# Sliding-window attention with a feed-forward stage: weights loaded and decoded in 16 parts of 1024 columns instead of 32 parts of 512

## The chip, the cores and the metric

One core of a Trainium2 chip runs the kernel. The metric is device time in microseconds (us) of one execution; lower is better. The engines of the core are TensorE (PE, with its weight loads PEld), VectorE (DVE), ScalarE (ACT), GpSimd (POOL) and SyncE (SP); here SP only issues DMAs, in order, and a DMA that waits holds back all that stand behind it on SP.

## The reference

```python
# attention, B=4, H=8, S=768, D=64, n_sink=4, window=128
scores = scale * np.matmul(q, k.transpose(0, 1, 3, 2))
keep = is_sink | in_window                       # rel = query - key, 0 <= rel < window
scores = np.where(keep, scores, -1000000000.0)
a = softmax(scores)
x = (a @ v).transpose(0, 2, 1, 3).reshape(3072, 512)
# feed-forward, d_model 512, d_ff 2048
h = x @ w_in
g = h * np.clip(h + 3.0, 0.0, 6.0) / 6.0
out = g @ w_out                                  # 3072 x 512 float32
```

The two weights w_in (512 x 2048) and w_out (2048 x 512) come as 64-bit floats, and the kernel itself turns each number into two 32-bit halves, a rounded high part and the rest (hi and lo).

## The kernel before

**Units.** A unit is one batch and 256 queries; there are 12 (4 batches, 3 stretches of queries). In the list `pus` each unit stands with each of its 4 pairs of heads, 48 entries s in all. The first stretches of all batches come first (entries 0 to 15). The first 12 entries are plain: they multiply in one pass and need no split keys. From entry 12 on keys and queries are split and stacked: `B_k` writes the split keys to `kt` and copies them by four DMAs into the tile `K`, of which there is one.

**The slot loop.** For each s the string ORDER lists what the program issues: the loads of V (`V`), the scores of entry s-1 (`C0`, `C1`: PE sp, then DVE line 320), the product with V of entry s-2 (`E0`, `E1`: PE av), exp (`X`, ACT line 341), the loads of keys and queries two entries ahead (`L`), the normalisation (`N`, lines 328 and 330), `Bk`, `Bq`, the weights (`W`), and the transposes (`D0`, `D1`: PE pt, ACT pf). At every `-` one step of the feed-forward stage is drained from `queues`. I call one turn of this loop a slot.

**The feed-forward stage.** When all four pairs of a unit are done, 34 steps are queued. For each of 8 groups i of 256 hidden columns: two halves of `ffn1` (PE hps, line 461; behind the second half ACT line 467, DVE lines 468, 41 and 470 make gf, gh and g), and two `ffn2` (PE o, line 481). A step is only issued when the weights of its group have been issued.

**The weights.** Group i needs `WIH[i]`, `WIL[i]` (from w_in) and `WOH[i]`, `WOL[i]` (from w_out), which stay in SBUF. `load_part` fetches one part by a DMA into a buffer st, and decodes it by a chain that changes engine three times: ACT line 153 (st to wt) and line 157 (st in place), DVE line 159 (st in place) and line 161 (wt from wt and st, after which st is free), ACT line 35 (hi from wt) and DVE line 164 (lo from wt and hi, after which wt is free). There are 32 parts of 128 x 512 numbers, 512 KB each, four for each group. st has four buffers (three with the tag st and one with the tag vs), wt three. WN says how many parts each slot issues: 1 in each of slots 1 to 4, 4 in each of slots 5 to 11. The result tile ost of `ffn_out` shares the tag st.

The order of instructions on each engine is fixed when the kernel is built, by a scheduler that works on the program's order and its own costs; on the chip each engine runs its list in order.

Of the kernel before, what the change touches and what calls it, by code (L numbers as in the profile page):

```python
# [9 lines left out]
F32 = mybir.dt.float32  # L10
F32R = mybir.dt.float32r
I32 = mybir.dt.int32
# [6 lines left out]
P = 128  # L19
# [7 lines left out]
def split_parts(nc, hi, lo, src, hi_engine, lo_engine):  # L27

    copy_r(nc, hi_engine, hi, src)
    lo_engine.tensor_tensor(out=lo, in0=src, in1=hi.bitcast(F32), op=ALU.subtract)  # L30


def copy_r(nc, eng, out, src, scale=1.0):
    if eng is nc.scalar:
        nc.scalar.mul(out=out, in_=src, mul=scale)  # L35
    elif eng is nc.gpsimd:
        nc.gpsimd.tensor_scalar(out=out, in0=src, scalar1=scale, scalar2=1.0, op0=ALU.mult, op1=ALU.mult)
    elif scale != 1.0:
        nc.vector.tensor_scalar(out=out, in0=src, scalar1=scale, scalar2=None, op0=ALU.mult)
    else:  # L40
        nc.vector.tensor_copy(out=out, in_=src)  # L41
# [3 lines left out]
def attn_ffn_kernel(ctx: ExitStack, tc: tile.TileContext, qx, kx, vx, vfx, vsx, n_sink, window, w_in, w_out, out):  # L45
    nc = tc.nc
    B, NU, NP = qx.shape[0:3]
    NT, DM = out.shape
    NFP = w_in.shape[0]
# [7 lines left out]
    work = fast.enter_context(tc.tile_pool(name="work", bufs=2))  # L57
# [66 lines left out]
    WIH = [const.tile([P, NP, 256], F32R, name=f"wih{i}") for i in range(NFP)]  # L124
    WIL = [const.tile([P, NP, 256], F32R, name=f"wil{i}") for i in range(NFP)]
    WOH = [const.tile([P, 2, DM], F32R, name=f"woh{i}") for i in range(NFP)]
    WOL = [const.tile([P, 2, DM], F32R, name=f"wol{i}") for i in range(NFP)]
# [3 lines left out]
    def weng(which, at):  # L131
        return {"D": nc.vector, "P": nc.gpsimd, "A": nc.scalar}[which[at % len(which)]]

    def load_part(hi, lo, src, rows, at):

        def like(t):
            return t.rearrange("p (a b) -> p a b", a=rows)

        if not wide:
            st = like(work.tile([P, 512], F32, tag="st", name="st", bufs=3))  # L140
            nc.sync.dma_start(out=st, in_=src)
            split_parts(nc, hi, lo, st, nc.scalar, nc.vector)
            return

        tag, bufs = ("vs", 1) if at % 4 == 3 else ("st", 3)
        st = work.tile([P, 512, 2], I32, tag=tag, name="st", bufs=bufs)
        it = work.tile([P, 512], I32, tag="wt", name="wt", bufs=3)
        nc.sync.dma_start(out=like(st.rearrange("p n w -> p (n w)")), in_=src.bitcast(I32))
        low, high = st[:, :, 0], st[:, :, 1]
        ft = it.bitcast(F32)  # L150


        nc.scalar.activation(out=ft, in_=high.bitcast(F32), func=AF.Abs, scale=2.0 ** -112)

        nc.scalar.activation(out=low, in_=low.bitcast(U32), func=AF.Copy, scale=2.0 ** -29 * (1 - 2.0 ** -18),  # L157
                             bias=7.5 * 2.0 ** -18 - 0.5)
        nc.vector.scalar_tensor_tensor(out=low, in0=high, scalar=-2 ** 31, in1=low,
                                       op0=ALU.bitwise_and, op1=ALU.bitwise_or)  # L160
        nc.vector.scalar_tensor_tensor(out=it, in0=it, scalar=3, in1=low,
                                       op0=ALU.logical_shift_left, op1=ALU.bitwise_or)
        copy_r(nc, weng(WHI, at), hi, like(ft))
        weng(WLO, at).tensor_tensor(out=lo, in0=like(ft), in1=hi.bitcast(F32), op=ALU.subtract)  # L164

    def load_w_in(i, c):
        cs = slice(2 * c, 2 * c + 2)
        load_part(WIH[i][:, cs, :], WIL[i][:, cs, :], w_in[i, :, cs, :], 2,
                  4 * i + c)

    def load_w_out(i, c):
        cs = slice(c, c + 1)
        load_part(WOH[i][:, cs, :], WOL[i][:, cs, :], w_out[i, :, cs, :], 1,
                  4 * i + 2 + c)

# [28 lines left out]
    def eng(which, s):  # L206
        return {"D": nc.vector, "P": nc.gpsimd, "A": nc.scalar}[which[1 + (s % (len(which) - 1)) if s < START else 0]]
# [242 lines left out]
    def ffn1(x, i, pool, psum, half, state, tag):  # L450

        if half == 0:
            state["h"] = psum.tile([P, 2, UT], F32, tag=tag or "hps", name="hps")
        hp = state["h"]
        fs = slice(P * half, P * (half + 1))
        n = 3 * NP
        j = 0
        for c in range(NP):
            xh, xl = x[c]
            for l, r in ((WIH[i][:, c, fs], xh), (WIH[i][:, c, fs], xl), (WIL[i][:, c, fs], xh)):  # L460
                nc.tensor.matmul(out=hp[:, half, :], lhsT=l, rhs=r, start=(j == 0), stop=(j == n - 1))  # L461
                j += 1
        if half == 1:
            g = pool.tile([P, 2, UT], F32R, tag="g", name="g", bufs=2)
            gh = pool.tile([P, 2, UT], F32R, tag="gh", name="gh", bufs=2)
            gf = pool.tile([P, 2, UT], F32, tag="gf", name="gf", bufs=2)
            nc.scalar.activation(out=gf, in_=hp, func=AF.Relu, bias=three, scale=1.0)  # L467
            nc.vector.scalar_tensor_tensor(out=gf, in0=gf, scalar=6.0, in1=hp, op0=ALU.min, op1=ALU.mult)  # L468
            copy_r(nc, eng(GHI, state["n"] * NP), gh, gf)
            eng(GLO, state["n"] * NP).tensor_tensor(out=g, in0=gf, in1=gh.bitcast(F32), op=ALU.subtract)  # L470
            state[i] = (gh, g)

    def ffn2(i, tt, psum, state, tag):
        if i == 0:
            state[f"o{tt}"] = psum.tile([P, DM], F32, tag=tag or f"o{tt}", name=f"o{tt}")
        gh, gl = state[i]
        acc = state[f"o{tt}"]
        ts_ = slice(P * tt, P * (tt + 1))
        for f in range(2):
            for j, (l, r) in enumerate(((gh, WOH), (gh, WOL), (gl, WOH))):  # L480
                nc.tensor.matmul(out=acc, lhsT=l[:, f, ts_], rhs=r[i][:, f, :],  # L481
                                 start=(i == 0 and f == 0 and j == 0),
                                 stop=(i == NFP - 1 and f == 1 and j == 2))

    def ffn_out(tt, pool, state, dst):
        o = pool.tile([P, DM], F32, tag="st", name="ost", bufs=3)
        nc.scalar.mul(out=o, in_=state[f"o{tt}"], mul=1.0 / 6.0)
        nc.sync.dma_start(out=dst, in_=o)

    def ffn_steps(n, x, pool, psum_h, psum_o, dsts, tag=None):  # L490

        state = {"n": n}
        steps = []
        for i in range(NFP + 1):
            if i < NFP:
                for half in range(2):
                    steps.append((4 * i + 2, lambda i=i, half=half: ffn1(x, i, pool, psum_h, half, state, tag)))
            if i >= 1:
                for tt in range(2):
                    steps.append((4 * i, lambda i=i, tt=tt: ffn2(i - 1, tt, psum_o, state, tag)))  # L500
        steps.append((0, lambda: ffn_out(0, pool, state, dsts[0])))
        steps.append((0, lambda: ffn_out(1, pool, state, dsts[1])))
        return steps
# [5 lines left out]
    def drain(n):  # L509

        for _ in range(n):
            live = [q for q in queues if q]
            if not live:
                return
            if live[0] is queues[0] and len(live) > 1:
                order = live[0:2]
            else:
                order = live[0:1]
            for q in order:
                if q[0][0] <= 4 * NFP - len(w_order):  # L520
                    q.pop(0)[1]()
                    break

    w_order = []
    for i in range(NFP):
        for c in range(2):
            w_order.append(lambda i=i, c=c: load_w_in(i, c))
        for c in range(2):
            w_order.append(lambda i=i, c=c: load_w_out(i, c))

    PRE = 0
    for _ in range(PRE):
# [6 lines left out]
    def slot_E(s, h):  # L539
        if 0 <= s < NS:  # L540
            E_av(s, h)
            b, u, p = pus[s]
            if h == 1 and p == NP - 1:
                r0 = b * S + u * UT
                dsts = [out[r0 + P * tt:r0 + P * (tt + 1), :] for tt in range(2)]
                queues.append(ffn_steps(units.index((b, u)), xt[(b, u)], work, ps, ps, dsts, "bank"))

    ORDER = "V C0 - C1 E0 X - E1 L - N - Bk - Bq W - D0 - S D1 -"
    MULT = [1] * 12
    WN = [0, 1, 1, 1, 1, 4, 4, 4, 4, 4, 4, 4]  # L550

    for s in range(NS + 2):
        if s == 3:
            later_constants()
        for step in ORDER.split():
# [23 lines left out]
            elif step == "W":  # L579
                for _ in range(WN[s] if s < len(WN) else 0):  # L580
                    with ExitStack() as behind:
                        if s <= 5:
                            at = max(min(s, NP) - 2, 0)
# [176 lines left out]
```

## Time and profile before

| | |
|---|---|
| median of 3 runs | 748.91 us (747.79 to 750.85) |
| the profiled execution | 751.12 us, its span 749.3 us |
| PE | 727.1 us busy, 97% of the span |
| DVE | 477.9 us busy, 64% |
| ACT | 445.9 us busy, 60% |
| DMA, HBM read | 42.21 MB over the span |

The profiled execution is 2.2 us above the median; 1.8 us of it lie outside its span. Busy times are unions: matmuls overlap in the array, so PE counts as busy while a single late matmul drains. A row of the timeline gives the start, the duration, the engine, the line, what it writes and reads, the shape and how many were merged; in brackets stands how long the engine had been idle before and what released it. [...]

### The profile page before, as it was taken

The numbers are of one execution on the slowest core, as the hardware profiler recorded it, in microseconds if no ns is written. First come the engines' busy times: TensorE is split into PE (matmuls) and PEld (weight loads), VectorE is DVE, ScalarE is ACT, GpSimd is POOL, SyncE is SP. The second block draws the span as 40 slices with busy tenths as digits, with TensorE's granted clock in tenths as the row PEclk, the third lists the DMA queues.
The fourth block names the chain that finished last, engine by engine and source line by source line (L and its number), as shares of the span: only waits on it lengthen the run. The fifth ranks groups of instructions, "written<-read, shape, count | busy, mean of one in ns | idle before, by whom it ended". The sixth has DMA issues, their size and how long they took to land.

```text
span 749.3 us, 13811 instructions
## 1 busy us (share of the span) xinstructions
PE 727.1 (97%) x4932; PEld 653.4 (87%) x4932; DVE 477.9 (64%) x1306; ACT 445.9 (60%) x1099; POOL 4.0 (1%) x17
## 2 busy tenths in 40 slices
PE   8998999999999999999999999999999999999996
PEld 7776878999989998988999889999899889999895
DVE  5798986467767657666756766765766675533321
ACT  6989886556667566666556665756655754411111
POOL 1000000000000000000000000000000000000000
PEclk9999999999999999999999999999999999999999
DMA  7666654336445355345434535535534532000000
GB/s 241 194 205 220 199 173 106 110 81 155 112 123 166 87 127 155 101 114 156 105 98 131 141 101 132 156 87 131 151 102 103 154 83 59 30 1 1 29 1 32
DMA packets 53549, 87.25 MB, mean 116 GB/s; under 512 B 8160, under 2 KB 36320, under 8 KB 53472
## 3 DMA queue, kind: packets, MB, share of 16 engines
q1 hardware_dynamic: 53328, 86.28, 41.9%
q8 instruction: 41, 0.67, 0.4%
q14 instruction: 36, 0.29, 0.1%
q10 hardware_dynamic: 144, 0.00, 0.0%
HBM read 42.21 MB, written 6.29 MB: 65 GB/s over the span
## 4 chain that ended last, share of the span: by engine, by line
PE 69%; ACT 12%; DVE 10%; DMA 5%; issue 2%; SPq 1%; ACTq 0%; DVEq 0%
PE o L481 28%; PE hps L461 27%; PE av L423 5%; PE pt L365 4%; PE sp L313 3%; ACT Pt L328 2%; ACT Pt L341 2%; DMA st<-in_w_in_dram 2%; ACT Ph L341 1%; DVE gf L468 1%; DVE g L470 1%; ACT gf L467 1%; DMA K<-kt 1%; DVE Pt L320 1%; ACT st L157 1%
## 5 line engine op out<-in xcount | busy, mean ns | idle before, releaser
L461 PE MATMUL hps<-xh,wih 128*128 128x256 f32 x768 | 221.0, 288 | 3.6 <-ACT wih L35 3.3
L461 PE MATMUL hps<-xh,wil 128*128 128x256 f32 x768 | 218.0, 284 | 0.0
L461 PE MATMUL hps<-xl,wih 128*128 128x256 f32 x768 | 216.9, 282 | 0.1
L481 PE MATMUL o<-woh,gh 128*128 128x512 f32 x384 | 155.9, 406 | 5.6 <-DVE rc L344 2.3
L481 PE MATMUL o<-woh,g 128*128 128x512 f32 x384 | 153.1, 399 | 1.4 <-DVE g L470 0.9
L461 PEld LDWEIGHTS hps<-xh,wih 128*128 128x128 f32 x768 | 145.0, 189 | 8.9 <-ACT wih L35 6.3
L481 PE MATMUL o<-wol,gh 128*128 128x512 f32 x384 | 151.6, 395 | 0.0
L461 PEld LDWEIGHTS hps<-xl,wih 128*128 128x128 f32 x768 | 145.2, 189 | 2.0 <-issue 0.3
L461 PEld LDWEIGHTS hps<-xh,wil 128*128 128x128 f32 x768 | 145.1, 189 | 0.8 <-DVE wil L164 0.3
L468 DVE SCALAR_TENSOR_TENSOR gf<-gf,hps 128x512 f32<-128x512 f32 x96 | 65.9, 687 | 101.8 <-ACT gf L467 100.7
L467 ACT ACTIVATE gf<-hps,three 128x512 f32<-128x512 f32 x96 | 65.4, 681 | 91.7 <-PE hps L461 91.3
L341 ACT ACTIVATE Pt<-Pt,nb 128x272 f32<-128x272 f32 (+2 forms) x144 | 73.4, 510 | 59.9 <-DVE nb L320 58.5
L481 PEld LDWEIGHTS o<-woh,g 128*128 128x128 f32 x384 | 72.3, 188 | 22.4 <-DVE g L470 5.9
L481 PEld LDWEIGHTS o<-woh,gh 128*128 128x128 f32 x384 | 72.7, 189 | 18.0 <-DVE gh L41 3.4
L481 PEld LDWEIGHTS o<-wol,gh 128*128 128x128 f32 x384 | 72.7, 189 | 10.9
L328 ACT ACTIVATE Pt<-Pt,rc 128x272 f32<-128x272 f32 (+2 forms) x144 | 66.0, 506 | 18.4 <-DVE rc L344 18.3
L470 DVE TENSOR_TENSOR g<-gf,gh 128x512 fp32r<-128x512 f32 x96 | 66.1, 689 | 1.4
L320 DVE CUSTOM_DVE_ANT_0 Pt<-sp,m_t 128x272 f32<-128x272 f32 x128 | 52.3, 438 | 20.7 <-PE sp L313 19.9
L30 DVE TENSOR_TENSOR pl<-pt,ph 128x512 fp32r<-128x512 f32 (+1 forms) x72 | 48.4, 674 | 16.8 <-ACT ph L35 16.3
L35 ACT ACTIVATE ph<-pt 128x512 fp32r<-128x512 f32 (+1 forms) x72 | 42.1, 585 | 19.5 <-PE pt L365 17.2
L313 PE MATMUL sp<-K,Q 128*128 128x272 f32 (+2 forms) x288 | 47.3, 288 | 0.4 <-DMA Q<-qt 0.4
L313 PEld LDWEIGHTS sp<-K,Q 128*128 128x128 f32 x288 | 42.2, 189 | 3.6 <-DMA Q<-qt 0.6
(92 smaller groups left out, 927.9 us busy)
## 6 DMA issues: line engine op xcount, KB each, us to landing
K<-kt SPq DMA_DIRECT2D x128, 200.0 KB, 3.5
Q<-qt SPq DMA_DIRECT2D x144, 64.0 KB, 2.5
st<-in_w_in_dram SPq DMA_DIRECT2D x16, 512.0 KB, 4.0
st<-in_w_out_dram SPq DMA_DIRECT2D x16, 512.0 KB, 5.0
kr<-in_kx_dram SPq DMA_DIRECT2D x32, 200.0 KB, 2.5
qr<-in_qx_dram SPq DMA_DIRECT2D x48, 128.0 KB, 2.2
out_dram<-ost SPq DMA_DIRECT2D x24, 256.0 KB, 2.1
vr<-in_vx_dram SPq DMA_DIRECT2D x32, 192.0 KB, 2.6
```

What stands on the lines that cost most here:

```text
L30: lo_engine.tensor_tensor(out=lo, in0=src, in1=hi.bitcast(F32), op=ALU.subtract)
L35: nc.scalar.mul(out=out, in_=src, mul=scale)
L313: nc.tensor.matmul(out=sp[g][:, 0:w], lhsT=d["Q"][:, g, ts], rhs=d["K"][:, g, part, ks], start=(part == 0), stop=(part == 1))
L320: d["min"] = nc.vector.tensor_tensor_reduce(out=cell(s, g, t, 0, w), in0=sp[g][:, 0:w], in1=m[:, 0:w], scale=-SCALE, scalar=3.0e38, op0=AL ...
L328: nc.scalar.mul(out=blk, in_=blk, mul=c)
L341: d["exp"] = nc.scalar.activation(out=blk, in_=blk, func=AF.Exp, scale=-1.0, bias=d["nb"][:, i:i + 1], accum_out=d["sm"][:, i:i + 1])
L423: nc.tensor.matmul(out=o, lhsT=l, rhs=r, start=(j == 0 and (h == 0 or not plain(s))), stop=(j == len(seq) - 1 and (h == 1 or not plain(s))))
L461: nc.tensor.matmul(out=hp[:, half, :], lhsT=l, rhs=r, start=(j == 0), stop=(j == n - 1))
L467: nc.scalar.activation(out=gf, in_=hp, func=AF.Relu, bias=three, scale=1.0)
L468: nc.vector.scalar_tensor_tensor(out=gf, in0=gf, scalar=6.0, in1=hp, op0=ALU.min, op1=ALU.mult)
L470: eng(GLO, state["n"] * NP).tensor_tensor(out=g, in0=gf, in1=gh.bitcast(F32), op=ALU.subtract)
L481: nc.tensor.matmul(out=acc, lhsT=l[:, f, ts_], rhs=r[i][:, f, :], start=(i == 0 and f == 0 and j == 0), stop=(i == NFP - 1 and f == 1 and ...
```

## The change

The weights come in 16 parts of 128 x 1024 numbers, 1 MB each, two for each group (`load_w_in(i)` and `load_w_out(i)`). Each decode instruction works on 1024 columns and there are half as many. st has two buffers: one with the tag st (the w_in parts) and one in the place of the tile `K` (the w_out parts). wt has three buffers of double size: two with the tag wt and one with the tag vs. ost goes to the tag wt. WN and the conditions for draining count parts of the new size: slot 1 issues w_in of group 0, slot 3 w_out of group 0, slots 5 to 11 both parts of groups 1 to 7.

```diff
+        tag = ("st", "K")[at % 2]
         if not wide:
-            st = like(work.tile([P, 512], F32, tag="st", name="st", bufs=3))
+            st = like(work.tile([P, 1024], F32, tag=tag, name="st", bufs=1))
...
-        tag, bufs = ("vs", 1) if at % 4 == 3 else ("st", 3)
-        st = work.tile([P, 512, 2], I32, tag=tag, name="st", bufs=bufs)
-        it = work.tile([P, 512], I32, tag="wt", name="wt", bufs=3)
+        wtag, bufs = ("vs", 1) if at % 3 == 2 else ("wt", 2)
+        st = work.tile([P, 1024, 2], I32, tag=tag, name="st", bufs=1)
+        it = work.tile([P, 1024], I32, tag=wtag, name="wt", bufs=bufs)
...
-    def load_w_in(i, c):
-        cs = slice(2 * c, 2 * c + 2)
-        load_part(WIH[i][:, cs, :], WIL[i][:, cs, :], w_in[i, :, cs, :], 2,
-                  4 * i + c)
-
-    def load_w_out(i, c):
-        cs = slice(c, c + 1)
-        load_part(WOH[i][:, cs, :], WOL[i][:, cs, :], w_out[i, :, cs, :], 1,
-                  4 * i + 2 + c)
+    def load_w_in(i):
+        load_part(WIH[i], WIL[i], w_in[i], NP, 2 * i)
+
+    def load_w_out(i):
+        load_part(WOH[i], WOL[i], w_out[i], 2, 2 * i + 1)
...
-        o = pool.tile([P, DM], F32, tag="st", name="ost", bufs=3)
+        o = pool.tile([P, DM], F32, tag="wt", name="ost", bufs=2)
...
-                    steps.append((4 * i + 2, lambda i=i, half=half: ffn1(x, i, pool, psum_h, half, state, tag)))
+                    steps.append((2 * i + 1, lambda i=i, half=half: ffn1(x, i, pool, psum_h, half, state, tag)))
...
-                    steps.append((4 * i, lambda i=i, tt=tt: ffn2(i - 1, tt, psum_o, state, tag)))
+                    steps.append((2 * i, lambda i=i, tt=tt: ffn2(i - 1, tt, psum_o, state, tag)))
...
-                if q[0][0] <= 4 * NFP - len(w_order):
+                if q[0][0] <= 2 * NFP - len(w_order):
...
-    WN = [0, 1, 1, 1, 1, 4, 4, 4, 4, 4, 4, 4]
+    WN = [0, 1, 0, 1, 0, 2, 2, 2, 2, 2, 2, 2]
```

The file is three lines shorter behind this place: the decode lines 153, 157, 159, 161 and 164 become 154, 158, 160, 162 and 165, and later lines lose three (341 becomes 338, 328 becomes 325, 461 becomes 458).

The start of ACT's list before, from the first exp of entry 0 to the first hi of the weights (wih; Ph are the scores, pf the transposed ones):

```order
L341 ACTIVATE Ph,sm<-Ph,nb 128x256
L153 ACTIVATE wt<-st 128x512
L328 ACTIVATE Ph<-Ph,rc 128x256 x2
L157 ACTIVATE st<-st 128x512
L35 ACTIVATE pf<-pt 128x384 x2
L153 ACTIVATE wt<-st 128x512
L341 ACTIVATE Ph,sm<-Ph,nb 128x128
L35 ACTIVATE wih_111<-wt 128x512
```

The same place with the change:

```order
L338 ACTIVATE Ph,sm<-Ph,nb 128x256
L154 ACTIVATE wt<-st 128x1024
L325 ACTIVATE Ph<-Ph,rc 128x256 x2
L158 ACTIVATE st<-st 128x1024
L35 ACTIVATE pf<-pt 128x384 x2
L338 ACTIVATE Ph,sm<-Ph,nb 128x128 x2
L338 ACTIVATE Ph,sm<-Ph,nb 128x256
L35 ACTIVATE wih_111<-wt 128x1024
```

The first decode step stands at the same place, ahead of the normalisation of entry 0 (line 328, now 325), and now needs the whole first 1 MB; the second L153 of this stretch has left it, and three of the next four exps stand ahead of the first hi.

A stretch of the load stage on ACT before, group 4 (wih_115 and woh_131 are the high parts of its w_in and w_out), behind the exps of its slot:

```order
L153 ACTIVATE wt<-st 128x512
L157 ACTIVATE st<-st 128x512
L153 ACTIVATE wt<-st 128x512
L328 ACTIVATE Ph<-Ph,rc 128x256 x2
L35 ACTIVATE wih_115<-wt 128x512
L157 ACTIVATE st<-st 128x512 x2
L153 ACTIVATE wt<-st 128x512
L35 ACTIVATE wih_115<-wt 128x512
L35 ACTIVATE pf<-pt 128x384 x2
L157 ACTIVATE st<-st 128x512
L153 ACTIVATE wt<-st 128x512
L35 ACTIVATE woh_131<-wt 128x512 x2
```

The same slot on ACT with the change, from the two exps that open it to its last hi:

```order
L338 ACTIVATE Ph,sm<-Ph,nb 128x128 x2
L154 ACTIVATE wt<-st 128x1024
L464 ACTIVATE gf<-hps,three 128x512
L338 ACTIVATE Ph,sm<-Ph,nb 128x256 x2
L35 ACTIVATE xh_842<-av 128x256
L158 ACTIVATE st<-st 128x1024
L325 ACTIVATE Ph<-Ph,rc 128x256 x2
L154 ACTIVATE wt<-st 128x1024
L158 ACTIVATE st<-st 128x1024
L35 ACTIVATE wih_115<-wt 128x1024
L35 ACTIVATE pf<-pt 128x384 x2
L35 ACTIVATE woh_131<-wt 128x1024
```

And on DVE in the same slot, the decode of group 4 (wil_123 and wol_139 are the low parts):

```order
L160 SCALAR_TENSOR_TENSOR st<-st 128x1024
L162 SCALAR_TENSOR_TENSOR wt<-wt,st 128x1024
L160 SCALAR_TENSOR_TENSOR st<-st 128x1024
L165 TENSOR_TENSOR wil_123<-wt,wih_115 128x1024
L162 SCALAR_TENSOR_TENSOR wt<-wt,st 128x1024
L317 ISA Ph,nb<-sp,m_100 128x128
L317 ISA nb 128x1
L317 ISA Ph,nb<-sp,m_100 128x128
L317 ISA nb 128x1
L165 TENSOR_TENSOR wol_139<-wt,woh_131 128x1024
```

Before, ACT's list of a slot held twelve decode steps of 512 columns between the same rows of attention, those of four parts in turn, so that one part's steps stood between another's; now it holds six of 1024, and on ACT only the two pf stand between the hi of w_in and that of w_out, which needs DVE's second L162.

## Rows read from the trace of the kernel before

**Rows 1.** From the page: the chain of work that ended last, shares of the span by engine and by line.

```profile
PE 69%; ACT 12%; DVE 10%; DMA 5%; issue 2%; SPq 1%; ACTq 0%; DVEq 0%
PE o L481 28%; PE hps L461 27%; PE av L423 5%; PE pt L365 4%; PE sp L313 3%; ACT Pt L328 2%; ACT Pt L341 2%; DMA st<-in_w_in_dram 2%; ACT Ph L341 1%; DVE gf L468 1%; DVE g L470 1%; ACT gf L467 1%; DMA K<-kt 1%; DVE Pt L320 1%; ACT st L157 1%
```

**Rows 2.** Busy time by stretch. Columns: the stretch, its length, busy us and instructions of PE, PEld, DVE, ACT and POOL in this order, the granted clock, the DMA share and GB/s.

```profile
20.00:40.00 20.00, 18.16 (x129) 15.02 (x128) 16.52 (x53) 19.96 (x56) 0.00 (x0) 1.00 0.61 189
...
60.00:80.00 20.00, 18.73 (x109) 15.08 (x109) 18.08 (x45) 18.53 (x43) 0.00 (x0) 0.91 0.62 204
80.00:100.00 20.00, 19.27 (x132) 16.91 (x130) 18.03 (x46) 18.03 (x44) 0.00 (x0) 1.00 0.60 199
...
120.00:140.00 20.00, 20.00 (x124) 16.89 (x123) 10.64 (x35) 12.04 (x35) 0.95 (x1) 1.00 0.38 107
```

**Rows 3.** The start: SP's issue of the first two weight loads, the time from issue to landing of the loads issued from 4.8 to 5.3 us (two) and of the one issued at 6.23 us (the fourth), and ACT's first decode step and PE's first transposes in the timeline.

```profile
4.91 0.80 SPq L148 DMA_DIRECT2D st<-in_w_in_dram  x2
DMA to landing us min/median/max: 5.1/5.6/6.2
DMA to landing us min/median/max: 7.8/7.8/7.8
10.32 0.64 ACT L153 ACTIVATE wt<-st 128x512 f32<-128x512 f32 x1
11.30 1.03 PE L365 MATMUL pt<-ident_r,Ph 128*128 128x128 f32 x6 [0.81 <-DVE Ph L330]
```

**Rows 4.** Timeline, decode steps back to back, first on ACT, then on DVE.

```profile
36.80 0.70 ACT L157 ACTIVATE st<-st 128x512 int32<-128x512 uint32 x1
37.38 0.69 ACT L153 ACTIVATE wt<-st 128x512 f32<-128x512 f32 x1
37.95 0.68 ACT L157 ACTIVATE st<-st 128x512 int32<-128x512 uint32 x1
38.51 0.62 ACT L35 ACTIVATE wih<-wt 128x512 fp32r<-128x512 f32 x1
39.03 0.87 ACT L35 ACTIVATE pf<-pt 128x384 f32<-128x384 f32 x2
39.77 0.69 ACT L157 ACTIVATE st<-st 128x512 int32<-128x512 uint32 x1
...
38.60 0.69 DVE L159 SCALAR_TENSOR_TENSOR st<-st 128x512 int32<-128x512 int32 x1
39.20 0.69 DVE L164 TENSOR_TENSOR wil<-wt,wih 128x512 fp32r<-128x512 f32 x1
39.81 0.69 DVE L161 SCALAR_TENSOR_TENSOR wt<-wt,st 128x512 int32<-128x512 int32 x1
```

**Rows 5.** Groups of instructions from 26 to 113 us with shapes kept apart. Columns: line, engine, operation, names, shapes, count, busy us, mean ns, idle time before them and its releasers.

```profile
L35 ACT ACTIVATE wih<-wt 128x512 fp32r<-128x512 f32 x13 | 8.1, 621 | 0.0
L35 ACT ACTIVATE xh<-av 128x256 fp32r<-128x256 f32 x6 | 2.2, 370 | 0.0
L164 DVE TENSOR_TENSOR wil<-wt,wih 128x512 fp32r<-128x512 f32 x13 | 9.0, 690 | 3.0 <-ACT wih L35 3.0
L439 DVE TENSOR_TENSOR xl<-av,xh 128x256 fp32r<-128x256 f32 x6 | 2.5, 413 | 0.0
```

**Rows 6.** Timeline of ACT, the other work of a slot back to back (exps of 128 and 256 columns, xh, normalisation).

```profile
30.87 0.40 ACT L341 ACTIVATE Ph<-Ph,nb 128x128 f32<-128x128 f32 x1
...
31.25 0.51 ACT L341 ACTIVATE Ph<-Ph,nb 128x256 f32<-128x256 f32 x1
...
31.74 0.51 ACT L341 ACTIVATE Ph<-Ph,nb 128x256 f32<-128x256 f32 x1
...
32.24 0.37 ACT L35 ACTIVATE xh<-av 128x256 fp32r<-128x256 f32 x1
32.50 0.66 ACT L157 ACTIVATE st<-st 128x512 int32<-128x512 uint32 x1
33.05 0.91 ACT L328 ACTIVATE Ph<-Ph,rc 128x256 f32<-128x256 f32 x2
33.85 0.68 ACT L153 ACTIVATE wt<-st 128x512 f32<-128x512 f32 x1
```

**Rows 7.** Timeline of ACT, the fifth and the thirteenth of the sixteen hi steps of w_in, which are the first ones of groups 2 and 6.

```profile
49.29 0.62 ACT L35 ACTIVATE wih<-wt 128x512 fp32r<-128x512 f32 x1
...
99.57 0.62 ACT L35 ACTIVATE wih<-wt 128x512 fp32r<-128x512 f32 x1
```

**Rows 8.** Loads: the page's row on the w_in loads (issues, KB each, median us to landing), the landing of the one load issued from 58.5 to 60 us, and SP's longest wait up to 135 us (total us, times, longest).

```profile
st<-in_w_in_dram SPq DMA_DIRECT2D x16, 512.0 KB, 4.0
DMA to landing us min/median/max: 6.1/6.1/6.1
SPq L148 <- DVE wt L161: 42.5, 21, 4.0
```

**Rows 9.** A gap of PE in the timeline, and busy time by stretch of 2 us around it (columns as in Rows 2).

```profile
59.02 0.47 PE L481 MATMUL o<-woh,gh 128*128 128x512 f32 x1 [2.33 <-DVE rc L344]
...
62.00:64.00 2.00, 2.00 (x8) 1.44 (x7) 2.00 (x4) 2.00 (x6) 0.00 (x0) 0.56 0.10 33
64.00:66.00 2.00, 2.00 (x15) 1.51 (x15) 2.00 (x5) 1.80 (x5) 0.00 (x0) 1.00 0.73 249
```

**Rows 10.** Timeline of DVE at the end of the load stage: the last L161, then the low part of the first split keys.

```profile
120.00 0.69 DVE L161 SCALAR_TENSOR_TENSOR wt<-wt,st 128x512 int32<-128x512 int32 x1
120.60 0.42 DVE L30 TENSOR_TENSOR kt<-kr,kt 128x256 fp32r<-128x256 f32 x1
```

More of the change, by code (lines that the diff above doesn't have):

```diff
@@ L525, in attn_ffn_kernel @@
     for i in range(NFP):
[L526 to L529, printed above, removed]
+        w_order.append(lambda i=i: load_w_in(i))
+        w_order.append(lambda i=i: load_w_out(i))
     PRE = 0
```

## The prediction

> **What bounds the kernel now.** I read the page first, then busy time by stretch, the waits, and the timelines of ACT, DVE and SP up to 130 us. The chain that ended last is 69% PE, nearly all of it the two feed-forward products [rows 1]. From 120 us on PE is never idle, while DVE and ACT are idle nearly half the time [rows 2]: the weights are decoded by then, and nothing in the change touches that work. What is left is the load stage, from 5 to about 120 us. There ACT is full first (19.96 of 20 us from 20 to 40), and then ACT and DVE are both busy 18 of 20 us [rows 2]. PE looks busy there too, but a late matmul counts until it has drained, and it does only 109 matmuls in a stretch of 20 us where 124 fit later. So I take the end time as the moment at which the weights and the first units are ready, plus a remainder that does not change: each us by which the load stage ends earlier or later is a us of the total.
>
> **What an instruction of 1024 columns costs.** Back to back, ACT starts a decode step of 512 columns every 0.57 us (36.80 to 37.38 to 37.95), a hi every 0.52, DVE a step every 0.60, though each lasts longer, 0.62 to 0.69 [rows 4]: the end of one lies under the start of the next. Per column I take the difference between 256 and 512 columns: (621 - 370)/256 = 0.98 ns on ACT, (690 - 413)/256 = 1.08 ns on DVE [rows 5]. 512 columns are thus 0.50 us of ACT's 0.57 and 0.55 of DVE's 0.60. The other steps run at about 1.04 ns a column if the pitch has little else in it. I take a pitch of 1.10 (ACT decode), 1.03 (hi) and 1.13 (DVE), and a duration 0.1 longer. One merged step then saves ACT some 0.03 us and DVE 0.07. Over 48 merges that is 1.4 and 3.4 us of engine time; per slot of six merges 0.2 and 0.4.
>
> [...]
>
> **The start: later.** The first two loads were issued at 4.91 and 5.28 us and landed 5.1 and 6.2 us later, at 10.0 and 11.5; the fourth, issued at 6.23, landed at 14.0 [rows 3]. They come one behind the other, about 1.35 us for 512 KB. With the change the first 1 MB is what the first two loads were: it lands at 11.5. ACT was ready for its first decode step at 10.32 [rows 3] and now waits 1.2 us, with the normalisation of entry 0 (line 325) and so PE's first transposes (11.30) behind it. Then the first hi: ACT reaches it after L158, two pf and three exps, at about 16.7 us by the pitches of [rows 4, 6]. DVE needs L160 and L162 behind L158 with an exp's score between them, 14.6 + 1.2 + 0.3 + 1.2 = 17.3. That is another 0.6 to 0.7 us. ACT has no other idle time up to 40 us to hide this in [rows 2]. Against it stand about 12 merges up to there, 12 x 0.03 = 0.4. The start costs 1.2 + 0.7 - 0.4 = 1.5 us.
>
> **A slot: the same.** I walk one slot with the lists of the change, from the end of ACT's L158 on w_in (time 0).
> - DVE: L160, L162, at 2.4 done; st of w_in is free.
> - ACT meanwhile: normalisation 0.80, L154 and L158 of w_out 2.2, so 3.0; hi of w_in from 3.0 to 4.1, two pf to 4.8.
> - DVE: L160 of w_out can start at 3.1, lo of w_in at 4.3, L162 of w_out at 5.4, done 6.7.
> - ACT: the hi of w_out must wait for it, from 4.8 to 6.7 (idle 1.9), and ends at 7.8.
> - ACT: two exps of 128 columns (0.385 each) to 8.5, L154 of the next w_in to 9.6, Relu 0.57 to 10.2, two exps of 256 (0.49) to 11.2, xh 0.27, L158 from 11.45 to 12.65.
>
> So 12.65 us a slot. Before, group 2 to group 6 took (99.57 - 49.29)/4 = 12.57 us a slot, waits included [rows 7]. The saved pitches are eaten by the hi of w_out, which has no other part's steps to fill its wait. Five such slots make +0.4 us; in the last two slots two units' feed-forward steps share the engines and PE is nearly full (19.27 of 20 us [rows 2]), and I count nothing. Bounds: if the work alone counts, -0.4 x 7 = -2.9; upwards, the load. A w_in part's buffer is free at 2.4 and its next contents are wanted at 8.5, so a load has 6.1 us. 512 KB of w_in landed in 4.0 us in the median [rows 8], so 1 MB is 4.0 + 1.35 = 5.4 us, 0.7 to spare. From the slowest load of that stage, 6.1 [rows 8], it is 7.5, which would cost 1.4 us in a slot.
>
> **What else moves.** On SP a load of weights holds keys, queries and V behind it as before (SP waited 42.5 us for L161 [rows 8]); keys are fetched two entries, some 25 us, ahead, and that covers it. The tile K is free when the last L162 is done. Before, the split keys (kt) stood right behind the last L161 on DVE anyway, 120.00 and 120.60 [rows 10], so the copies into K gain no wait; without that cover they would be late by one step, 1.1 us. ost finds wt long free. These cost nothing, nor does the third wt.
>
> **Sum.** +1.5 for the start and +0.4 for the slots on the profiled 751.12 us is 753.0; that execution is 2.2 us above the median, so 750.8 us against 748.91. A measurement of this kernel can tell about 0.5%, 3.7 us, from no change.
>
> **Rivals.**
> - *The merges pay in full.* If each step's fixed part is what its duration shows beyond the columns, 0.12 us on ACT (621 - 512 x 0.98) and 0.14 on DVE [rows 5], 48 merges save 5.8 us of ACT. Less 1.9 for the start, 748.9 - 3.9 = 745.0. For it: both engines are near full, and the chains of decode wait on each other's ends, not on pitches. Against it: [rows 4]. [...]
> - *Two buffers are too few.* The load takes 7.5 us and every second transfer is late: 1.4 us in each of six reloads of w_in, +8.4 to the +1.9, 759. For it: SP already waits for L161 more than for anything else. Against it: DMAs have idle time in every stretch (0.60 to 0.62 busy [rows 2]) and a part is loaded nearly alone. It decides once 1 MB takes over 6.1 us.
> - *PE gaps and its clock.* With whole groups arriving at once PE waits longer between hps and o. [...]
>
> **How the numbers follow.** Forecast 0.5 (its own range 747 to 752.6), the merges in full 0.2, two buffers 0.15, the clock 0.15. Faster by over 0.5% (below 745.2) is mostly the first rival, 0.2; slower (above 752.7) the other two, 0.3; between them 0.5. The range reaches from 744.5, just under the first rival, to 757, above the clock and short of the full price of the buffers: about 0.2 is left out.
>
> **What would show it.** The changed profile should have ACT's first L154 start at about 11.5, the hi of w_out preceded by an idle time of 1 to 2 us that DVE's L162 ends, ACT waiting for no load of w_in in the slots, and 12 to 13 us between the hi steps of two groups. The forecast is wrong if ACT waits for DMAs in most slots, if PE's clock falls in more than two stretches, or if the slot comes out under 12 us.

## The result, and the profile after

The changed kernel takes 753.74 us, the median of 22 runs (750.55 to 756.09); the kernel before took 748.86 us in 22 runs beside it (747.32 to 753.27). The ratio is 1.0051, with a 95% interval of 1.0038 to 1.0063: 2.8 to 4.7 us slower (the two medians alone differ by 4.9). The profiled execution took 753.41 us, its span 751.6 us.

The page, the chain of work that ended last by engine, and the two groups of weight loads (issues, KB each, median us to landing):

```profile
PE 71%; DVE 11%; ACT 10%; DMA 4%; issue 2%; SPq 1%; ACTq 0%; DVEq 0%
...
st<-in_w_in_dram SPq DMA_DIRECT2D x8, 1024.0 KB, 5.0
st<-in_w_out_dram SPq DMA_DIRECT2D x8, 1024.0 KB, 4.9
```

The chain is nearly that of [rows 1]. A load of w_in of 1 MB took 1.0 us longer than one of 512 KB [rows 8], a load of w_out no longer than before:

```profile
st<-in_w_out_dram SPq DMA_DIRECT2D x16, 512.0 KB, 5.0
```

Busy time by stretch (columns as in [rows 2]):

```profile
20.00:40.00 20.00, 19.85 (x107) 15.37 (x103) 12.62 (x44) 15.79 (x44) 0.00 (x0) 0.83 0.45 143
40.00:60.00 20.00, 19.78 (x124) 16.02 (x125) 17.11 (x35) 16.17 (x33) 0.00 (x0) 1.00 0.57 193
60.00:80.00 20.00, 13.83 (x78) 10.80 (x76) 18.29 (x38) 18.10 (x33) 0.00 (x0) 1.00 0.62 211
80.00:100.00 20.00, 19.84 (x141) 17.32 (x142) 18.61 (x40) 16.14 (x32) 0.00 (x0) 1.00 0.68 238
120.00:140.00 20.00, 20.00 (x122) 16.77 (x121) 10.77 (x31) 11.27 (x31) 0.00 (x0) 1.00 0.40 112
```

From 120 us on the pace is as before, as forecast. Two stretches lost: from 20 to 40 us ACT is busy for 15.79 us where it was full before, and PE does 107 matmuls instead of 129, at a granted clock of 0.83 (1.00 before); from 60 to 80 us PE does 78 instead of 109. The stretches between and behind them won a part of it back.

How far PE is at a time is the best measure of the loss. These are PE's matmuls, counted one by one in the traces, without those that compute nothing (L81: both kernels have some in their first entries, which keep PE busy); each trace holds 4832:

| begun by | 30 us | 60 us | 80 us | 130 us |
|---|---|---|---|---|
| before | 89 | 241 | 348 | 638 |
| changed | 62 | 230 | 306 | 626 |

12 matmuls at 130 us are some 1.8 us at the 6.8 a microsecond that PE does from there to the end; the spans differ by 2.3 us.

**The first place, 10 to 28 us.** SP, ACT, DVE and PE in the timeline; the load issued at 4.96 landed 5.4 us later:

```profile
4.96 0.33 SPq L149 DMA_DIRECT2D st<-in_w_in_dram  x1
...
10.37 1.11 ACT L154 ACTIVATE wt<-st 128x1024 f32<-128x1024 f32 x1
16.06 1.06 ACT L35 ACTIVATE wih<-wt 128x1024 fp32r<-128x1024 f32 x1 [0.54 <-DVE wt L162]
17.03 0.49 ACT L338 ACTIVATE Ph<-Ph,nb 128x256 f32<-128x256 f32 x1
...
17.15 1.22 DVE L165 TENSOR_TENSOR wil<-wt,wih 128x1024 fp32r<-128x1024 f32 x1 [0.78 <-ACT wih L35]
18.30 0.16 DVE L340 TENSOR_SCALAR sm<-sm 128x4 f32<-128x4 f32 x1
18.90 0.48 DVE L327 TENSOR_SCALAR Ph<-Ph,rc 128x128 f32<-128x128 f32 x2
...
19.25 0.52 PE L362 MATMUL pt<-ident_r,Ph 128*128 128x128 f32 x2 [1.97 <-DVE Ph L327]
```

The load is there when ACT wants it, though only just: it landed at 10.33, and ACT was free at 10.37. But the last exp of entry 1 now stands behind the whole first hi on ACT, and on DVE the sum of that exp (L340) stands behind the low part of 1024 columns. Entry 1's normalisation comes at 18.90, and PE waits 1.97 us for it. Before, it waited 0.39 us at this place:

```profile
16.86 0.71 PE L365 MATMUL pt<-ident_r,Ph 128*128 128x128 f32 x4 [0.39 <-DVE Ph L330]
```

In the changed kernel PE's clock then falls:

```profile
18.00:20.00 2.00, 0.75 (x6) 0.58 (x7) 1.40 (x7) 2.00 (x3) 0.00 (x0) 1.00 0.88 373
20.00:22.00 2.00, 2.00 (x12) 1.12 (x8) 1.95 (x7) 1.69 (x5) 0.00 (x0) 0.78 0.49 193
22.00:24.00 2.00, 2.00 (x7) 1.53 (x7) 1.60 (x4) 2.00 (x9) 0.00 (x0) 0.50 0.28 70
24.00:26.00 2.00, 2.00 (x11) 2.00 (x11) 0.71 (x4) 1.06 (x2) 0.00 (x0) 0.50 0.72 167
26.00:28.00 2.00, 2.00 (x10) 1.83 (x9) 0.00 (x0) 0.00 (x0) 0.00 (x0) 0.51 0.90 377
28.00:30.00 2.00, 2.00 (x13) 1.34 (x11) 0.81 (x4) 1.59 (x3) 0.00 (x0) 1.00 0.34 97
```

At a granted clock of 0.50 the matmuls of entry 2 that compute nothing take 3.6 us instead of 1.95, and ACT and DVE stand idle behind them from 26 to 28 us.

**The second place, 52 to 68 us.** In the timeline, SP's issue of group 3's w_in (it landed 6.0 us later), then on ACT its first step and the hi steps of w_in of groups 2, 3 and 5:

```profile
52.73 0.33 SPq L149 DMA_DIRECT2D st<-in_w_in_dram  x1
...
53.02 1.04 ACT L35 ACTIVATE wih<-wt 128x1024 fp32r<-128x1024 f32 x1
58.77 1.13 ACT L154 ACTIVATE wt<-st 128x1024 f32<-128x1024 f32 x1 [1.35 <-DMA st<-in_w_in_dram]
67.01 1.06 ACT L35 ACTIVATE wih<-wt 128x1024 fp32r<-128x1024 f32 x1 [0.35 <-DVE wt L162]
91.76 1.06 ACT L35 ACTIVATE wih<-wt 128x1024 fp32r<-128x1024 f32 x1
```

From group 2 to group 3 it is 14.0 us; then (91.76 - 67.01)/2 = 12.4 a slot. Before, the first halves of groups 2 and 3 stood at 49.29 [rows 7] and 59.02. PE starts the hidden products of groups 3 and 4 as soon as their hi steps are done, at 68.07 and 80.11, and waits for them (in the first row the profile names another releaser, but the hi is what ended last):

```profile
68.12 0.39 PE L458 MATMUL hps<-xh,wih 128*128 128x256 f32 x1 [1.48 <-DVE st L160]
...
80.16 0.39 PE L458 MATMUL hps<-xh,wih 128*128 128x256 f32 x1 [1.87 <-ACT wih L35]
```

### The profile page after: what moved, and what is told of

It is laid out like the page before. It is cut to its first block, busy times and chain, and to the rows that moved or that the text cites. A ratio compares the mean times of both kernels' runs of the same rounds, so it can differ in the third digit from the quotient of the medians.

```text
span 751.6 us, 13682 instructions
## 1 busy us (share of the span) xinstructions
PE 728.6 (97%) x4932; PEld 653.5 (87%) x4932; DVE 475.4 (63%) x1258; ACT 441.6 (59%) x1051; POOL 4.0 (1%) x17
## 4 chain that ended last, share of the span: by engine, by line
PE 71%; DVE 11%; ACT 10%; DMA 4%; issue 2%; SPq 1%; ACTq 0%; DVEq 0%
PE hps L458 28%; PE o L478 28%; PE av L420 5%; PE pt L362 4%; PE sp L310 3%; ACT Pt L325 2%; ACT Pt L338 2%; DMA st<-in_w_in_dram 1%; DVE gf L465 1%; DVE Pt L317 1%; DMA K<-kt 1%; PE sp L306 1%; DVE g L467 1%; ACT wt L154 1%; ACT Ph L338 1%
```

## The experiments

Each was timed against the kernel before on the same chip.

| kernel | runs | median us | before | ratio, 95% interval |
|---|---|---|---|---|
| changed, again | 12 | 754.43 | 748.89 | 1.0062 [1.0044, 1.0079] |
| changed, 8 matmuls at the start | 12 | 751.72 | 748.89 | 1.0035 [1.0021, 1.0050] |
| changed, group 0 in small parts | 6 | 757.15 | 748.89 | 1.0101 [1.0078, 1.0123] |
| before, parts issued together | 12 | 748.60 | 748.89 | 0.9994 [0.9973, 1.0015] |
| changed, decode in halves | 12 | 751.92 | 750.04 | 1.0018 [0.9998, 1.0038] |
| changed, 92 matmuls | 6 | 761.28 | 750.04 | 1.0160 [1.0131, 1.0188] |
| before, 84 matmuls | 6 | 761.18 | 750.04 | 1.0144 [1.0117, 1.0170] |
| changed, group 0 small, other buffers | 8 | 754.12 | 750.04 | 1.0056 [1.0035, 1.0078] |
| changed, third buffer | 12 | 749.82 | 749.57 | 0.9999 [0.9982, 1.0016] |
| the same, 8 matmuls at the start | 12 | 747.92 | 749.57 | 0.9972 [0.9958, 0.9986] |
| the same, and decode in halves | 6 | 745.70 | 749.57 | 0.9946 [0.9925, 0.9967] |
| before, 8 matmuls at one place | 12 | 745.98 | 749.57 | 0.9949 [0.9933, 0.9966] |

After the first result there were four theories: the clock at the start, the clock in the slots, the size of the decode instructions, and the loads (1 MB at once, two buffers).

**The changed kernel again.**

> The changed kernel once more, for a second profile. In its first profile PE stood idle for 1.97 us before the transposes of entry 1 (at 19.25 us), its granted clock then lay at 0.50 from 22 to 28 us, and the first feed-forward matmul came at 38.35 us against 31.05 before. Theory A (the start: that PE gap and the low clock behind it cost about 3.5 us): the gap is there again, and where the clock does not fall the first feed-forward matmul comes about 3.5 us earlier and the total is near 751; where it falls, 753 to 755. Theory B (whole groups decoded early stand ahead of attention, whatever the clock does): the first feed-forward matmul at 35 to 38 us and 753 to 754 us in either case.

The loss is there again, 1.0062. The profiled execution, at 756.82 us the slowest of the twelve, started in another way: its first load took 7.2 us, and ACT waited for it:

```profile
12.75 1.12 ACT L154 ACTIVATE wt<-st 128x1024 f32<-128x1024 f32 x1 [1.70 <-DMA st<-in_w_in_dram]
```

This is the wait that the prediction had priced at 1.2 us. Of the eight profiles of kernels whose first load has 1 MB, it is the only one that has it; in the other seven that load landed 5.2 to 5.5 us after its issue. PE's gaps at the start here were 1.53 us (ending at 14.32) and 1.34 us (23.97), and its first hidden product came at 40.3 us, later than either theory had it. The clock fell in three places, at 14 to 22, 66 to 70 and 82 to 88 us (to 0.50, 0.51 and 0.50), so this profile does not tell the theories apart.

Where the clock falls differs between executions of one program; over all runs the mean granted clock of the span was 0.9921 for the changed kernel (34 runs) and 0.9961 for the kernel before (77 runs). Run by run the time follows it: straight lines through these runs give 0.5 us (changed) and 0.7 us (before) more for each 0.001 less of the clock. At the same clock, 0.996, the lines stand at 751.6 and 749.8 us, some 1.8 us apart. So about half of the loss goes with the lower clock, wherever in the execution it falls, and about half does not; this is read from how the runs differ, and is not a test.

**Filling the gap at the start.**

```diff
             elif step[0] == "D" and 0 <= s - 1 < NS:
+                if s == 2 and step == "D0":
+                    keep_busy(8)
```

> The changed kernel with 8 more filler matmuls (1.95 us at the full clock) in front of the transposes of entry 1, where PE stood idle for 1.97 us. They do no part of the result and delay nothing that was ready. Theory A: PEclk stays at 1.00 from 20 to 30 us, the fillers of the next entry take 1.95 instead of 3.62 us, the first feed-forward matmul comes at about 35 us, and the total is 2.5 to 3.5 us under the changed kernel, about 750.5. Theory B: the clock stays up, but the total does not move by more than 1 us (753 to 754), since the decode work ahead of attention sets the start.

The 8 matmuls are the only difference in the order of any engine, so this is the cleanest of the tests: what the other edits move, they move together with the order that the scheduler writes. Its busy time by stretch:

```profile
18.00:20.00 2.00, 1.81 (x15) 1.38 (x15) 1.43 (x6) 2.00 (x3) 0.00 (x0) 1.00 0.99 414
22.00:24.00 2.00, 2.00 (x16) 1.95 (x17) 1.75 (x6) 2.00 (x10) 0.00 (x0) 1.00 0.44 125
26.00:28.00 2.00, 2.00 (x12) 1.19 (x12) 0.94 (x6) 2.00 (x6) 0.00 (x0) 1.00 0.96 381
```

The clock stays at 1.00 and ACT is full again from 26 to 28 us. The mean clock of its runs is 0.9961, the same as before the change. The ratio falls to 1.0035 from 1.0051 and 1.0062: the gap at the start, with the clock behind it, is 1.2 to 2.0 us of the loss, and 2.6 us (0.0035 x 749) have another cause.

**Group 0 in small parts, twice.** Group 0 in 4 parts of 512 columns in entries 1 to 4, as before the change, the rest in parts of 1024.

```diff
+        n = 1024
+        if small is not None:
+            n, tag = 512, ("st", "K", "vs", "st")[small]
```

> The changed kernel with group 0 in four parts of 512 columns, one in each of slots 1 to 4 as before, and groups 1 to 7 in parts of 1024. It leaves the start as before and keeps the slots of the change. Theory A and B: the loss lies in the start, so 748 to 750 us (the slots took 12.4 us each in both kernels). Theory C (the loss lies in the slots: two buffers, and the hi of w_out that waits for DVE): 752 to 754, and the first feed-forward matmul near 31 us nevertheless.

This was no clean test: the fourth small part holds a load buffer until 29 us, group 1 came late, and the time rose to 757.15. In the second version the small parts take st, vs, K and vs:

> The changed kernel with group 0 alone in 4 parts of 512 columns, issued in entries 1 to 4 as before the change, in buffers that do not hold back group 1 (the single one, the place of the sink values, the place of the keys, the place of the sink values again); groups 1 to 7 in parts of 1024. If the start is where the loss is, the first hidden product stands near 31 us again and the time is 749 to 750.5. If the slots are, it is 752 to 754.

The first hidden product stands at 31.11 us, as before the change, but PE then waits 3.00 us for group 1 (35.59 to 38.59). By 60 us PE has begun 237 matmuls, by 80 us 306, no more than in the changed kernel, and the time is 754.12. The early first product was worth nothing here, since PE was not fed afterwards.

**The order of issue alone.** The kernel before, with both halves of w_in, and of w_out, issued in one entry:

```diff
-    WN = [0, 1, 1, 1, 1, 4, 4, 4, 4, 4, 4, 4]
+    WN = [0, 2, 0, 2, 0, 4, 4, 4, 4, 4, 4, 4]
```

> The kernel before with its parts of 512 columns, but those of group 0 issued two by two in slots 1 and 3, as the change issues them, instead of one by one in slots 1 to 4. Theory B (what counts is that a whole half group is decoded in one slot, ahead of attention): 751 to 754, first feed-forward matmul later than 33 us. If the size of the instruction counts (DVE cannot put a short step of attention between halves), 748 to 750.

748.60 against 748.89: that both halves arrive together costs nothing that is seen. It has a gap at the start too (1.70 us, ending at 18.99), with the clock at 1.00 behind it in this execution; the mean clock of its runs, 0.9963, is that of the kernel before beside it. So most of the longer gap (0.39 before, 1.70 here, 1.97 with the change) comes with the order of issue, and a gap by itself does not yet cost time.

**The size of the instructions.** Loads of 1 MB in two buffers as in the change, each part decoded in two halves (inside `load_part`, `r2 = rows // 2`). The edit also puts wt in four buffers of 512 columns in place of three of 1024, and gives the result tile ost four in place of two:

```diff
+        for c in range(2):
+            it = work.tile([P, 512], I32, tag="wt", name="wt", bufs=4)
+            low, high = st[:, 512 * c:512 * c + 512, 0], st[:, 512 * c:512 * c + 512, 1]
+            hc, lc = hi[:, r2 * c:r2 * c + r2], lo[:, r2 * c:r2 * c + r2]
...
```

> The changed kernel with its 16 loads of 1 MB in two buffers, but each part is decoded in two halves of 512 columns, all six steps of the first half ahead of those of the second; only the size of the decode instructions goes back. If the loss lies in the size of the instructions (a value waits for a step of twice the length, the low part of 1024 columns stands ahead of entry 1's normalisation), this comes back to 749 to 750.5 and the gap ahead of entry 1's transposes shrinks from 1.97 us to under 1.7. If it lies in the loads (1 MB at once, two buffers), it stays at 753 to 754.5. The separate pitches of twice as many instructions cost at most 1 to 3 us in the second case.

The ratio is 1.0018 [0.9998, 1.0038], no longer told apart from the kernel before. Undoing the merge takes back 2.5 to 3.3 us (1.0051 or 1.0062 less 1.0018, times 749; by the intervals each of the two is uncertain by about 2). It does so although the mean clock of these runs, 0.9938, is still below the 0.9953 of the kernel before beside them. The gap at the start was 1.70 us in this profile, just short of what was expected, and behind it ACT waited 2.33 us for PE, until 28.01 (3.35 us at this place in the changed kernel, with the clock at 0.50); the mean clock of this execution was 0.989. The loads of 1 MB, which are still there, cost nothing that can be told from noise (the interval reaches to 2.9 us).

**Extra matmuls throughout.** 84 in all: 6 matmuls that compute nothing, ahead of each first half of the hidden product and each first tile of the output product of unit 0, groups 0 to 6.

```diff
+            for _ in range(6 if state["n"] == 0 and i < NFP - 1 else 0):
+                nc.tensor.matmul(out=state["h"][:, 0, 0:P], lhsT=ident, rhs=ident, start=True, stop=True)
...
+        if state["n"] == 0 and tt == 0 and i < NFP - 1:
+            keep_busy(6)
```

> The changed kernel with extra matmuls that compute nothing: 8 ahead of entry 1's transposes, as before, and 6 ahead of each first half of the hidden product and of each first token tile of the output product of unit 0, groups 0 to 6. If the low clock after PE's gaps is the loss in the slots too, the granted clock stays near 1.00 from 12 to 120 us and the time comes to 749 to 750. If the loss is that the weights come later, the clock stays up and the time stays at 751 to 752.5, as with the 8 matmuls alone; the extra matmuls are some 10 us of PE in gaps, and any of them that stands where PE has work makes it longer.

> The kernel before with the same extra matmuls that compute nothing ahead of unit 0's feed-forward steps, groups 0 to 6, and none at the start. Its own profile had two low-clock stretches, from 60 to 64 and from 110 to 116 us. If these cost it as much as the changed kernel's cost that one, it comes to 746 to 747.5, and the distance to the changed kernel with extra matmuls is what the later weights cost by themselves. If PE's gaps there are free, it stays at 748.5 to 749.5; above 750 the extra matmuls are in the way.

Neither theory's time came; it is the case that the expectations named last, matmuls in the way. In the changed kernel the clock was 1.00 from 40 to 100 us, in each stretch of 20 us, and yet it took 9.4 us more than with the 8 matmuls alone (1.0160 less 1.0035, times 749); before the change the extra matmuls cost 10.8 us (0.0144 x 750). 84 of them at 0.24 us (8 take 1.95) are 20.5 us of PE: about half went into gaps, and the other half stood in the way of work. So the runs tell nothing on the clock by itself. The two kernels are now 1.2 us apart (1.0160 against 1.0144), where the changed kernel with the 8 matmuls alone was 2.6 us above the kernel before: that agrees with a loss that goes by way of PE's gaps, but the intervals leave room for a distance of about 4 us, so it is not shown.

**A third load buffer.** st takes turns in three buffers; group 7's products read group 6's low parts to make room, so they also no longer wait for low parts of their own.

```diff
-        tag = ("st", "K")[at % 2]
+        tag, sb = (("st", 2), ("st", 2), ("K", 1))[at % 3]
...
+    WIL.append(WIL[-1])
```

> The changed kernel with a third load buffer of 1 MB, used in turn. To make room, group 7's products read group 6's low parts, and group 7's low parts are computed as before but into the scratch tile; the number of instructions is the same. In the changed kernel the load of group 3's w_in was issued only at 52.73 us and ACT waited 1.35 us for it, and PE fell behind between 60 and 80 us. If the two buffers are what costs there, the hi of group 3's w_in comes to 63 to 64.5 us (67.01 before), the useful matmuls done by 80 us to 320 or more (298), and the time to 751 to 752. If they cost nothing, 753 to 754.5 as with the change.

In the timeline, SP's issue of group 3's w_in, its hi on ACT, and the last hi of all:

```profile
42.06 0.33 SPq L152 DMA_DIRECT2D st<-in_w_in_dram  x1
...
57.79 1.05 ACT L35 ACTIVATE wih<-wt 128x1024 fp32r<-128x1024 f32 x1
105.97 1.06 ACT L35 ACTIVATE woh<-wt 128x1024 fp32r<-128x1024 f32 x1 [0.64 <-DVE wt L165]
```

And its busy time by stretch:

```profile
20.00:40.00 20.00, 19.84 (x133) 15.91 (x132) 15.12 (x46) 19.03 (x49) 0.00 (x0) 1.00 0.58 200
60.00:80.00 20.00, 18.00 (x114) 14.66 (x113) 19.04 (x38) 18.68 (x37) 0.00 (x0) 1.00 0.69 241
```

The load is issued 10.7 us earlier, the hi comes at 57.79 (expected at 63 to 64.5, 67.01 with two buffers), PE has begun 354 matmuls by 80 us (306 in the changed kernel, counted as above), and the time is 749.82, below what was expected: 3.9 to 4.7 us less than with two buffers. The last weights are ready 14.8 us earlier (105.97 against 120.73), so most of that gain is not on the path. The gap at the start is there unchanged (1.98 us) and the clock did not fall behind it in this execution (1.00 from 20 to 40 us).

> The same third buffer and substitute low parts, and the 8 extra matmuls ahead of entry 1's transposes. If the clock at the start and the two buffers are the whole loss, this is the time before the change, 748.5 to 749.5. If the size of the decode instructions costs by itself as well, it stays 1.5 to 2.5 us above it, 750.5 to 751.5.

> Third buffer, substitute low parts and the 8 extra matmuls again, and the decode in halves of 512 columns; what is left of the change is loads of 1 MB. If the size of the instructions costs, this is 1.5 to 2.5 us faster than the run with whole parts, 748.5 to 749.5, the same as before the change. If it does not, the two agree within 0.5 us.

The 8 matmuls at the start are worth 2.0 us again (0.9999 to 0.9972), the halves another 1.9 (0.9972 to 0.9946). Both runs came out faster than either theory had said: the third buffer gives more than the theories had allowed for. It is more room than the kernel before had (3 MB of loads in place of 2), so it shows that the load stage gains from more buffers, and not that the loss came from having two.

**One place in the kernel before.**

```diff
+        if state["n"] == 0 and tt == 0 and i == 2:
+            keep_busy(8)
```

> The kernel before with 8 extra matmuls at one place, ahead of unit 0's first output product of group 2, where its profile had the gap of 2.34 us (56.68 to 59.02) with the granted clock at 0.59 and 0.56 behind it. If that clock drop is a usual one and on the path, 747 to 748 and a mean granted clock of 0.997 or more; if not, 748.5 to 750.

The gap and the extra matmuls in PE's timeline (each of the 8 stands there as two rows):

```profile
59.19 0.77 PE L483 MATMUL o<-woh,gh 128*128 128x512 f32 x1 [2.33 <-DVE rc L344]
63.33 1.95 PE L81 MATMUL idle<-rel 128*128 128x128 f32 x16
```

And the stretch between:

```profile
60.00:62.00 2.00, 2.00 (x7) 1.51 (x7) 1.84 (x6) 2.00 (x5) 0.00 (x0) 0.50 0.87 308
```

It is the fastest kernel here that computes everything, 745.98 us, 0.9949 [0.9933, 0.9966], but not for the reason given: the matmuls came behind the gap, the clock fell all the same, and the mean clock of the runs is 0.9969 against 0.9962 for the kernel before beside it. The edit also changed the order that the scheduler wrote behind that place: 79 of the 1099 places in ACT's list and 85 of the 1306 in DVE's hold another instruction. Which of these gave the 3.8 us is open. It is as much as the whole loss under study, and it came from an edit that touches no load and no decode step: a new order alone may be worth that much.

## Why the prediction was right, and where it was not

The time, 753.74, lies in the stated range of 744.5 to 757. It lies above the forecast's own range of 747 to 752.6, in the part to which the prediction gave 0.3 for two rivals, and neither rival came as it was told. The loss is 2.8 to 4.7 us where 1.9 were forecast. The sign was right, and the slots were walked nearly right; that the sum came this near is in part luck, since its largest term mostly did not come and others were missing.

- **Each us of the load stage is a us of the total.** This premise of the sum fell. The last hi of w_out stands at the same time in the two profiles, before and after, and the spans differ by 2.3 us:

```profile
120.72 0.63 ACT L35 ACTIVATE woh<-wt 128x512 fp32r<-128x512 f32 x1 [3.00 <-DVE wt L161]
```

```profile
120.73 1.04 ACT L35 ACTIVATE woh<-wt 128x1024 fp32r<-128x1024 f32 x1
```

With the third buffer it stands 14.8 us earlier, and the time is 3.9 to 4.7 us less. What goes with the time is how many matmuls PE has done: by 130 us 638 before, 626 with the change, 667 with the third buffer.

- **The first load (+1.2).** This was wrong as a rule. The price of 1 MB was put together from two loads of 512 KB, one behind the other, the second landing at 11.5. In seven of eight profiles the one load landed 5.2 to 5.5 us after its issue, in the changed kernel's first profile at 10.33, and ACT's L154 starts at 10.37 with no wait. In its second profile the load took 7.2 us, and there the wait came, 1.70 us long. How often that happens is open.
- **The first hi (+0.7).** This was right: ACT waits 0.54 us for L162.
- **The merges (-0.4 at the start).** This was too small: ACT's steps of 1024 start 1.01 to 1.05 us apart (12.17 to 13.18, 18.79 to 19.81), not 1.10, DVE's 1.14 (1.13 taken). A merge saves ACT 0.1 us (2 x 0.57 - 1.03).
- **What stands behind the merged steps at the start.** This term was missing. The prediction asked only whom the first hi waits for, and not what waits for it: the exp behind it on ACT and the sum behind the low part on DVE. These lie ahead of PE's gap of 1.97 us, and filling that gap, which also kept the clock up, gave back 1.2 to 2.0 us. Most of the gap's length came with both halves arriving together (1.70 us with small steps), which the prediction did not ask either. The third rival looked for longer waits of PE, but between hps and o. The price that puts the clock near 757, the upper end of the range, is shown by no run: the mean clock says that (0.9961 - 0.9921) x 750 = 3.0 us at a clock of 1.00 were lost, which is 6 us more at 0.50, and by the lines through the runs that is worth 2 to 3 us of time. The prediction's sign of being wrong here, a low clock in more than two stretches, is met by the second profile and not by the first.
- **The slots (+0.4).** The walk gave 12.65 us a slot and the trace shows 12.4 from group 3 to 5, with the hi of w_out of groups 3 to 5 behind 0.63, 0.78 and 1.19 us of idle time that L162 ends (1 to 2 were foreseen). But the walk began in steady state, and the step from group 2 to 3 takes 14.0. DVE did group 2's L162 at 51.44, behind four scores, so the buffer was late, and the load of 6.0 us ended 1.35 us after ACT wanted it.
- **Two buffers are too few.** The rival's condition, a load above 6.1 us, was not met in the slots, and ACT waited for loads only 1.5 us in all in the first profile (4.1 us before the change):

```profile
ACT woh L35 <- DVE wt L162: 3.0, 4, 1.2
ACT wt L154 <- DMA st<-in_w_in_dram: 1.5, 2, 1.3
```

A third buffer gave 3.9 to 4.7 us nevertheless. The order of each engine is written ahead of time, and with the third buffer the steps of the load stage stand earlier in it, so the shortage hardly appears as a wait of ACT for a DMA; SP's own wait up to 122 us for the step that frees st is 41.3 us with two buffers and 31.5 with three. That ACT waits for no load was therefore a poor sign to look for.
- **The merges pay in full.** This rival fell: with two buffers or three, the merged steps are slower than halves, by 2.5 to 3.3 and by 1.9 us. It took 0.12 us of ACT for each merge, an estimate from [rows 5]; the trace has 0.1. A merged step gives the result for its first columns only when the whole step ends, and the next engine, the buffer and whatever is queued behind wait for it; at the start the rows above show this (the hi runs from 16.06 to 17.12, and DVE's low part, after 0.78 us without work, starts at 17.15), for the slots it is argued.

So undoing the merge takes back 1.9 to 3.3 us, and filling the gap at the start 1.2 to 2.0 us. The two overlap, since the long steps lengthen the gap (1.97 against 1.70 us), and they need not add up to the loss. No run shows a cost of the loads of 1 MB or of the order of issue. Of these edits only the 8 matmuls at the start leave every other instruction in its place, so that part is shown. The halves and the third buffer also bring a new order: even without the decode steps, 50 to 78 places in ACT's and DVE's lists hold another instruction than without the edit. The halves gained in two different orders, which speaks for the size of the steps; that nothing else in the new orders gained is not shown.

## What to carry to other kernels

When two engines hand a value to and fro, merging their steps saved a tenth of a microsecond a step here, and the handoff came later (DVE's first low part at 17.15 us instead of 14.76): ask of each merged step what is queued behind it on its own engine, above all where the pipeline fills. Where a scheduler writes the order, a shortage of buffers can show in when the steps stand and in the wait of the queue that issues the loads, with hardly a wait for a load (41.3 us of SP's beside 1.5 of ACT's here); add a buffer to find out. Any edit then also brings a new order, which can move the time as much as the edit itself: prefer a test that leaves the order alone. And of a gap of PE count the clock behind it too (0.50 behind 1.97 us in one execution here).

## What the runs showed of the hardware

- One load of 1 MB (8 KB for each partition) was mostly through sooner than two of 512 KB: 5.2 to 5.5 us after its issue in seven profiles and 7.2 us in one, while the second of two small ones, issued 0.4 us behind the first, took 6.2 us. From 8 to 10 us the queues moved 414 GB/s, against 305 with the small ones. The stretch in the changed kernel, then in the kernel before:

```profile
8.00:10.00 2.00, 2.00 (x20) 2.00 (x19) 1.30 (x9) 1.50 (x7) 0.49 (x3) 1.00 1.00 414
```

```profile
8.00:10.00 2.00, 2.00 (x21) 2.00 (x20) 1.25 (x9) 1.55 (x7) 0.45 (x3) 1.00 0.90 305
```
- The same gap does not always bring the low clock: behind 1.97 us it fell to 0.50, behind 1.98 (third buffer) and 1.70 us (parts issued together) it stayed at 1.00, and so it did in the changed kernel's own first profile behind a gap of 2.41 us that ended at 63.61. One profile is no measure of what the clock costs; the mean over the runs is a better one.
